# A chunk-selected attention and a gated feed-forward on one core: every engine's order written by a list scheduler, the feed-forward spread between heads, transposes by DMA later on, triangles on GpSimd

## The chip, the cores and the metric

The kernel runs on one core of one Trainium2 chip. The metric is the time of one execution in microseconds (us) on the device; smaller is better. Below, PE is TensorE, ACT ScalarE, DVE VectorE, POOL GpSimd and SP SyncE. PSUM is the memory that PE writes; it has eight banks of 512 float32 per partition, and no DMA and no POOL instruction touches it.

## The reference

Four batches, eight heads, 768 positions, head size 64. Each query takes the six best chunks of 32 keys, by an upper bound made of each chunk's smallest and largest key, and attends to them causally. The heads' outputs, side by side, are the input of a gated feed-forward layer that also mixes positions.

```python
B, H, S, D = q.shape                      # 4, 8, 768, 64
ub = np.sum(np.maximum(q[:, :, :, None, :] * k_min[:, :, None, :, :],
                       q[:, :, :, None, :] * k_max[:, :, None, :, :]), axis=-1)
top_chunks = np.argsort(ub, axis=-1)[..., -top_k:]          # 6 of 24, causal
scores = np.where(mask, scale * np.matmul(q, k.transpose(0, 1, 3, 2)), -1e9)
attn = softmax(scores);  x = heads side by side of attn @ v  # 768 x 512 a batch
h = np.maximum(x @ w_in, 0.0);  u, v = h[..., :512], h[..., 512:]
v_s = np.einsum('ts,bsd->btd', w_spatial, norm(v)) + b_spatial[None, :, None]
out = (u * v_s) @ w_out                                      # float32
```

## The kernel before

Work goes by **pairs** of heads: 16 pairs, four to a batch, a pair being 128 partitions wide (two heads of 64). For pair `i` there are three steps in the code.

- `load(i)` (L133): six DMAs on POOL's queue, two each for k, q and v, converted to float16 on the way.
- `prep(i)` (L148): PE transposes k (L152); DVE takes each chunk's maximum and minimum out of PSUM (L155, L156); ACT copies the transposed k into `kh` (L157, L158), whose other rows hold a constant pattern (made by POOL, L93 to L97, and copied by DVE, L107) that turns a chunk's selection bit into a large negative score; POOL lays out the chunk bounds `km` (L161). PE transposes q (L167), DVE splits it into positive and negative part (L169, L170), PE multiplies the bounds (L177), and DVE adds the causal mask (L180), takes the eight largest of each row (L186) and writes a bit for each chunk that isn't chosen beside q (L189). PE transposes this again (L196), and DVE copies it out as `a` (L198).
- `attend(i)` (L204), for each head: scores `sc` in three groups of up to two banks (L213), each diagonal block with a second matmul (L216) that adds a triangle `tri`; ACT's exp for each group (L217); the product with v (L224); DVE's normalisation (L227, L228). Then PE transposes the pair's output and DVE copies it into `xT` (L234, L235).

The feed-forward of a batch is a list of 21 pieces (L272 to L343): six `v_piece` (L285, ACT Relu L287, DVE statistics L289, L290), the norm (L295 to L299), four `u_piece` (L310, L312), four `s_piece` (positions mixed L322, the bias as one more matmul L324, the gate L325) and six `o_piece` (L333, copy L336, store on SP L337). Its pieces are issued after the pairs of the next batch, a share after each pair, and the last batch's after everything (L349 to L369). Within these, the framework's own scheduler sets each engine's order.

Each engine runs its instructions strictly in that order, so what stands behind a waiting instruction waits too. POOL's queue holds the loads, the weights' loads (L247) and `km`; a DMA of that queue also waits for the one eight before it. PSUM is shared out as two double banks `sc`, two `tr` and two `acc`.

Of the kernel before, what the change touches and what calls it, by code (L numbers as in the profile page):

```python
# [20 lines left out]

STRIPS = [
# [3 lines left out]
]  # L26
WIDTHS = [1024, 1024, 640]
BASES = [0, 1024, 2048]
EW = 2688


def block_column(t, qi):
    for g, strips in enumerate(STRIPS):
        for (tt, q0, n, col, _) in strips:
            if tt == t and q0 <= qi * P < q0 + n:
                return BASES[g] + col + qi * P - q0
    raise KeyError((t, qi))
# [3 lines left out]
def kernel(  # L41
# [24 lines left out]
    mm = nc.tensor.matmul  # L66

    cp = ctx.enter_context(tc.tile_pool(name="const", bufs=1))
    ring = ctx.enter_context(tc.tile_pool(name="ring", bufs=1))
    sb = ctx.enter_context(tc.tile_pool(name="sb", bufs=2))  # L70
    ml = ctx.enter_context(tc.tile_pool(name="ml", bufs=2))
    ps_sc = ctx.enter_context(tc.psum_pool(name="ps_sc", bufs=2))
    ps_tr = ctx.enter_context(tc.psum_pool(name="ps_tr", bufs=2))
    ps_acc = ctx.enter_context(tc.psum_pool(name="ps_acc", bufs=2))

    def trans_tile():
        return ps_tr.tile([P, S], F16, tag="tr", name="tr")
# [6 lines left out]
    identity = cp.tile([P, P], F16)  # L84
    make_identity(nc, identity)


    NB = 3
    qs_ring, kh_ring, v_ring = [], [], []
    expand = []  # L90
    for hi in range(2):
        ex = cp.tile([P, S], F16, name=f"expand{hi}")
        nc.gpsimd.memset(ex, NEG)  # L93
        row0 = 0 if hi == 0 else D
        nc.gpsimd.affine_select(out=ex, in_=ex, compare_op=Alu.is_ge, fill=0.0,
                                base=CHUNK * row0, channel_multiplier=-CHUNK, pattern=[[1, S]])
        nc.gpsimd.affine_select(out=ex, in_=ex, compare_op=Alu.is_ge, fill=0.0,  # L97
                                base=CHUNK - 1 - CHUNK * row0, channel_multiplier=CHUNK, pattern=[[-1, S]])
        expand.append(ex)
    for i in range(NB):  # L100
        qs = ring.tile([P, NQT, 2, P], F16, name=f"qs{i}")
        nc.vector.memset(qs, 0.0)
        qs_ring.append(qs)
        kh = []
        for hi in range(2):
            t = ring.tile([P, S], F16, name=f"kh{i}_{hi}")
            nc.vector.tensor_copy(t, expand[hi])  # L107
            kh.append(t)
# [9 lines left out]
    cmask = cp.tile([P, CPT], F32)  # L120
    nc.gpsimd.memset(cmask, 0.0)
    nc.gpsimd.affine_select(out=cmask, in_=cmask, compare_op=Alu.is_ge, fill=-1e9,
                            base=0, channel_multiplier=1, pattern=[[-CHUNK, CPT]])
    hmask = cp.tile([P, 2], F16)
    nc.gpsimd.memset(hmask, 0.0)
    nc.gpsimd.memset(hmask[0:D, 0:1], 1.0)
    nc.gpsimd.memset(hmask[D:2 * D, 1:2], 1.0)
    eps_t = cp.tile([P, 1], F32)
    nc.vector.memset(eps_t, 1e-6)

    kv = {}

    def load(i):  # L133
        b, hp = divmod(i, HP)
        qs, vt = qs_ring[i % NB], v_ring[i % NB]
        kp = sb.tile([P, NQT, 2, D], F16, tag="kp", name="kp", bufs=3)
        for hi in range(2):
            h = 2 * hp + hi
            view = lambda a: a[b, h].rearrange("(so si) d -> si so d", si=P)
            nc.gpsimd.dma_start(out=kp[:, :, hi, :], in_=view(k))  # L140
            c0 = D if hi == 0 else 0
            nc.gpsimd.dma_start(out=qs[:, :, hi, c0:c0 + D], in_=view(q))
            nc.gpsimd.dma_start(out=vt[:, :, hi, 0:D], in_=view(v))
        kv[i] = kp

# [254 lines left out]
```

## Time and profile before

| | us |
|---|---|
| median of three runs | 291.32 |
| lowest and highest | 287.43 and 292.05 |
| span of the profiled execution, first to last instruction | 287.5 |

The profiled execution has no other time of its own than its span. Its busy shares are PE 77%, DVE 59%, ACT 54%, POOL 34%. A busy PE counts a matmul to its modelled end, 0.16 us or so after the next one could start, so PE's real work is read from the steps between the starts of matmuls that follow each other.

### The profile page before, as it was taken

How to read it: one execution, taken by the hardware profiler on the slowest of the kernel's cores; microseconds unless marked ns; L12 is line 12 of the kernel's file. 1: busy time of each engine (PE TensorE's matmuls, PEld its weight loads, DVE VectorE, ACT ScalarE, POOL GpSimd, SP SyncE). 2: the span in 40 equal slices, each digit the busy share in tenths (PEclk: the TensorE clock that was granted, in tenths of full speed). 3: DMA queues.
4: the chain of work that ended last, by engine and by line, in shares of the span. 5: the costliest groups of instructions: out<-in, count | busy, mean ns of one | idle time of the engine just before them, and what ended most of it. 6: DMA issues, size and time to landing. Idle time of an engine off the chain costs nothing.

```text
span 287.5 us, 5812 instructions
## 1 busy us (share of the span) xinstructions
PE 222.4 (77%) x2340; PEld 144.9 (50%) x2340; DVE 170.7 (59%) x498; ACT 154.3 (54%) x217; POOL 98.1 (34%) x150
## 2 busy tenths in 40 slices
PE   0037028787879798989798989978888989799994
PEld 0025016666655565655465656655546565544551
DVE  8337005888788875565579865474688654238330
ACT  1021405775785868146878674086878660656213
POOL 9995264546562434124243424051200000000000
PEclk9999758999999999999999999999999999999999
DMA  0999997879996667558984848079220000140005
GB/s 1 65 120 199 194 127 52 56 49 71 70 65 41 46 41 47 37 64 65 204 55 31 55 31 57 0 81 222 16 15 3 0 2 0 39 182 2 0 0 219
DMA packets 80590, 18.86 MB, mean 66 GB/s; under 512 B 75698, under 2 KB 76978, under 8 KB 80564
## 3 DMA queue, kind: packets, MB, share of 16 engines
q0 software_dynamic: 77104, 12.20, 57.3%
q1 hardware_dynamic: 3460, 6.30, 6.0%
q8 instruction: 18, 0.29, 0.4%
q14 instruction: 8, 0.07, 0.1%
HBM read 24.39 MB, written 6.29 MB: 107 GB/s over the span
## 4 chain that ended last, share of the span: by engine, by line
PE 50%; ACT 23%; DMA 8%; POOL 7%; DVE 7%; issue 3%; ACTq 0%; DVEq 0%; POOLq 0%
ACT e L217 13%; PE acc L322 11%; PE sc L213 7%; PE acc L310 7%; DMA w_out_sb<-in_moe_w_out_dram 6%; PE acc L224 5%; PE acc L333 5%; PE acc L285 5%; DVE stats L289 2%; PE tr L234 2%; POOL kp L140 2%; PE sc L216 2%; DMA out_dram<-o 2%; ACT uT L312 2%; PE acc L324 2%
## 5 line engine op out<-in xcount | busy, mean ns | idle before, releaser
L217 ACT ACTIVATE e<-sc 128x1024 f16<-128x1024 f32 (+1 forms) x96 | 84.0, 916 | 44.0 <-PE sc L216 42.9
L140 POOL DMA_DIRECT2D kp<-in_k_dram x32 | 26.7, 839 | 54.1 <-PE tr L152 48.0
L224 PEld LDWEIGHTS <-e 128*128 128x128 f16 x672 | 27.0, 98 | 31.3 <-ACT e L217 17.8
L216 PE MATMUL sc<-tri,identity 128*128 128x128 f16 x192 | 39.5, 222 | 0.0
L336 ACT COPY o<-acc 128x512 f32<-128x512 f32 x24 | 14.0, 585 | 46.9 <-PE acc L333 44.8
L322 PE MATMUL acc<-wsT,vn 128*128 128x512 f16 (+1 forms) x192 | 37.2, 325 | 0.4 <-ACT uT L312 0.2
L325 DVE TENSOR_TENSOR gT<-acc,uT 128x512 f16<-128x512 f32 (+1 forms) x32 | 17.8, 557 | 20.0 <-PE acc L324 18.8
L155 DVE TENSOR_REDUCE kmm<-tr 128x24 f16<-128x768 f16 x16 | 15.3, 953 | 20.4 <-PE tr L152 20.3
L322 PEld LDWEIGHTS <-vn 128*128 128x128 f16 x192 | 18.2, 98 | 12.2 <-issue 1.1
L310 PE MATMUL acc<-xT,w_in_sb 128*128 128x512 f16 (+1 forms) x128 | 23.4, 325 | 0.9 <-ACT uT L312 0.7
L333 PE MATMUL acc<-w_out_sb,gT 128*128 128x512 f16 x96 | 23.1, 378 | 0.4 <-ACT o L336 0.3
L216 PEld LDWEIGHTS <-identity 128*128 128x128 f16 x192 | 19.0, 99 | 7.4 <-issue 5.7
L285 PE MATMUL acc<-w_in_sb,xT 128*128 128x512 f16 x96 | 22.2, 379 | 0.0
L177 PE MATMUL acc<-km,rq 128*128 128x48 f16 x160 | 9.6, 188 | 15.9 <-POOL km L161 14.5
L152 PE MATMUL tr<-identity,kp 128*128 128x128 f16 x96 | 10.0, 229 | 14.7 <-DMA kp<-in_k_dram 14.6
L312 ACT ACTIVATE uT<-acc 128x512 f16<-128x512 f32 (+1 forms) x32 | 14.3, 488 | 12.4 <-PE acc L310 12.3
L289 DVE BATCH_NORM_STATS2 stats<-vraw 128x6 f32<-128x512 f32 x24 | 16.6, 694 | 6.1 <-ACT vraw L287 6.1
L227 DVE RECIPROCAL rec<-acc 128x6 f32<-128x6 f32 x32 | 6.1, 190 | 22.9 <-PE acc L224 22.9
L287 ACT ACTIVATE vraw<-acc 128x512 f32<-128x512 f32 x24 | 14.3, 597 | 9.6 <-PE acc L285 9.6
L180 DVE TENSOR_TENSOR acc<-acc,cmask 128x40 f32<-128x40 f32 x16 | 3.3, 208 | 25.6 <-PE acc L177 22.7
L161 POOL TENSOR_TENSOR km<-kmm,hmask 128x48 f16<-128x48 f16 x32 | 8.3, 276 | 26.3 <-DVE kmm L155 22.6
L310 PEld LDWEIGHTS <-w_in_sb 128*128 128x128 f16 x128 | 12.1, 97 | 9.7 <-issue 1.3
(236 smaller groups left out, 452.0 us busy)
## 6 DMA issues: line engine op xcount, KB each, us to landing
out_dram<-o SPq DMA_DIRECT2D x24, 256.0 KB, 2.0
kp<-in_k_dram POOLq DMA_DIRECT2D x32, 96.0 KB, 3.3
qs_90<-in_q_dram POOLq DMA_DIRECT2D x12, 96.0 KB, 3.3
vt_96<-in_v_dram POOLq DMA_DIRECT2D x12, 96.0 KB, 3.0
ws_raw<-in_moe_w_spatial_dram POOLq DMA_DIRECT2D x1, 1152.0 KB, 15.1
w_in_sb<-in_moe_w_in_dram POOLq DMA_DIRECT2D x1, 1024.0 KB, 10.3
qs_98<-in_q_dram POOLq DMA_DIRECT2D x10, 96.0 KB, 3.2
vt_104<-in_v_dram POOLq DMA_DIRECT2D x10, 96.0 KB, 3.1
```

Source lines behind the costliest of these rows:

```text
L140: nc.gpsimd.dma_start(out=kp[:, :, hi, :], in_=view(k))
L213: mm(sc[:, col:col + n], lhsT=kh[hi][:, t * P:(t + 1) * P], rhs=a[hi][:, q0:q0 + n], start=True, stop=not dg)
L216: mm(sc[:, col:col + P], lhsT=identity, rhs=tri, start=False, stop=True)
L217: nc.scalar.activation(out=e[:, BASES[g]:BASES[g] + WIDTHS[g]], in_=sc[:, 0:WIDTHS[g]], func=Act.Exp, scale=scale)
L224: mm(avv[:, qi, :], lhsT=e[:, c:c + P], rhs=vt[:, t, hi, 0:D + 1], start=(t == 0), stop=(t == qi))
L285: mm(hv, lhsT=x[:, ko, bi * P:(bi + 1) * P], rhs=w_in_sb[:, ko, DH:DFF], start=(ko == 0), stop=(ko == NDO - 1))
L289: nc.vector.bn_stats(stats, st["vraw"][:, bi, :])
L310: mm(hu[:, 0:t1 - t0], lhsT=w_in_sb[:, ko, db * P:(db + 1) * P], rhs=x[:, ko, t0:t1], start=(ko == 0), stop=(ko == NDO - 1))
L312: nc.scalar.activation(st["uT"][:, db, t0:t1], hu[:, 0:t1 - t0], func=Act.Relu)
L322: mm(vs[:, 0:t1 - t0], lhsT=st["vn"][:, si, db * P:(db + 1) * P], rhs=wsT[:, si, t0:t1], start=(si == 0), stop=False)
L325: nc.vector.tensor_tensor(st["gT"][:, db, t0:t1], in0=vs[:, 0:t1 - t0], in1=st["uT"][:, db, t0:t1], op=Alu.mult)
L333: mm(o_ps, lhsT=st["gT"][:, db, ti * P:(ti + 1) * P], rhs=w_out_sb[:, db, :], start=(db == 0), stop=(db == KO - 1))
```

## The change

The file is rewritten. What is computed stays; these are its parts.

1. **Order.** Each piece of work is an operation with an engine, a length, a key, and names that it reads and writes. `Schedule.run` plays them through with these lengths: again and again it takes, over all engines, the operation that can start first, and among equals the one with the smallest key. That sequence is then issued, and the framework keeps it (`manual_schedule`). Eight single PSUM banks are handed out by it, with at most 3 for scores, 2 for transposes, 1 for bounds, 2 for outputs and 3 for the feed-forward at a time.
2. **Keys.** Pair `i` attends at `10 i`, is prepared at `10 i - 14` (the first at -50) and loaded at `10 i - 30`; the feed-forward of the batch whose last pair is `i` has V from `10 i + 16`, U from `+ 22`, S and O from `+ 30`.
3. **Loads.** A pair has four DMAs in place of six (k and v of both heads in one), and they come first on POOL, ahead of the constants. The weights are cut in nine and get keys 22 to 32, between the loads of pairs 5 and 6.
4. **Constants.** The pattern is made by DVE from the identity; DVE copies it to the rings' 64 rows.
5. **prep.** ACT copies transposed k once, whole (L378); DVE takes maxima and minima by a tree of two halvings and a reduction of 8 (L382 to L389) and places k in `kh` by four copies (L403). `km` is four small copies (L395), on DVE for the first two pairs and on POOL after. From pair 5 on, `a` comes from one DMA transpose on SP (L452) in place of 12 PE transposes and two DVE copies.
6. **attend.** Scores go by six groups of one bank, exp by six instructions. From pair 4 on no triangle is added by PE; POOL zeroes the triangles after exp, two instructions for a head (L501). The product with v comes in two parts (12 and 9 matmuls), started once for the whole bank. For pairs 4 to 14 a DMA transpose on SP writes `xT` (L530).
7. **Feed-forward.** U, and the mixed v, are computed with positions on the partitions; so the bias is a scalar for each partition in the gate (L602), and the bias matmuls and their preparation go. The gated tile must then be transposed: by DMA on SP for batches 0 to 2 (L606), by PE and DVE for the last (L613, L615).

```diff
+            for e, lst in ready.items():
+                for (k, n, t, o) in lst:
...
+                    t = max(t, free[e])
+                    if t < INF and (best is None or (t, k, n) < best[:3]):
+                        best = (t, k, n, e, o)
...
+    TRI_POOL = 4
+    A_XBAR = 5
+    PRE = 14
+    X_XBAR = 4
+    G_XBAR = 3
...
-        nc.vector.tensor_reduce(kmm[:, 0, :], trc, axis=AX.X, op=Alu.max)
-        nc.vector.tensor_reduce(kmm[:, 1, :], trc, axis=AX.X, op=Alu.min, negate=True)
-        nc.scalar.copy(kh[0][D:2 * D, :], tr[0:D, :])
-        nc.scalar.copy(kh[1][0:D, :], tr[D:2 * D, :])
+        s.op("ACT", *act_cost(S), lambda: nc.scalar.copy(kT, bk.f16[:, 0:S]), key, r=[bk], w=[("kT", n2)], drop=bk)
+            s.op("DVE", 0.26, 0.38, lambda m=m, op=op: nc.vector.tensor_tensor(
+                t1[:, m], in0=kc[:, :, 0:16], in1=kc[:, :, 16:32], op=op), key, r=[("kT", n2)], w=[("t1", n2, m)])
...
+                s.op("DVE" if i < 2 else "POOL", 0.2, 0.26, spread, key, r=[("kmm", n2, 0), ("kmm", n2, 1), ("kmz", n2)],
...
+        if i >= A_XBAR:
+            s.op("SP", 2.7, 4.7, lambda: nc.sync.dma_start_transpose(
+                out=a.rearrange("p t h c -> p (t h) c"), in_=qs.rearrange("p t h c -> p (t h c)")),
...
-                    if dg:
-                        mm(sc[:, col:col + P], lhsT=identity, rhs=tri, start=False, stop=True)
+                            dg = i < TRI_POOL and q0 == t * P
...
+                    nc.gpsimd.affine_select(out=o, in_=o, compare_op=Alu.is_ge, fill=0.0, base=0,
+                                            channel_multiplier=-1, pattern=[[0, 3], [1, P]])
+                if i >= TRI_POOL:
+                    s.op("POOL", *pool(3 * P), tri, kk, w=[("e", ne, 3 * part + j) for j in range(3)])
...
-                    mm(vs[:, 0:t1 - t0], lhsT=brow_l, rhs=brow[:, t0:t1], start=False, stop=True)
+            s.op("DVE", 0.61, 0.70, lambda t=t, bk=bk, g=g: nc.vector.scalar_tensor_tensor(
+                out=g, in0=bk.f32, scalar=bcol[:, t:t + 1], in1=u_r[nu[t]], op0=Alu.add, op1=Alu.mult),
...
+            if b < G_XBAR:
+                s.op("SP", 0.95, 3.0, lambda g=g, gT=gT: nc.sync.dma_start_transpose(out=gT, in_=g), kk,
...
+    weight_ops([22, 23, 26, 27, 28, 29, 30, 31, 32])
     for i in range(NPAIR):
+        load_ops(i, -101 if i == 0 else 10 * i - 30)
+        prep_ops(i, 10 * i - (PRE if i else 50))
+        attend_ops(i, 10 * i)
...
+            mlp_ops(b, k0, k0 + 6, k0 + 14, 1.0)
```

On POOL near the start of the program before, right behind the loads of the three weights, the second `km` row of pair 0 and the first of pair 1 stand with ten loads (`kp`, `qs_...`, `vt_...`) between them.

```order
L161 TENSOR_TENSOR km<-kmm,hmask 128x48 [waits DVE_49]
L140 DMA kp<-in_k_dram 128x6x64 [waits DMASW7_49]
L142 DMA qs_106<-in_q_dram 128x6x64 [waits DMASW0_49]
L143 DMA vt_112<-in_v_dram 128x6x64 [waits DMASW1_49]
L140 DMA kp<-in_k_dram 128x6x64 [waits DMASW2_49]
L142 DMA qs_106<-in_q_dram 128x6x64 [waits DMASW3_49]
L143 DMA vt_112<-in_v_dram 128x6x64 [waits DMASW4_49]
L140 DMA kp<-in_k_dram 128x6x64 [waits DMASW5_49,PE_49]
L142 DMA qs_90<-in_q_dram 128x6x64 [waits DMASW6_49,PE_49]
L140 DMA kp<-in_k_dram 128x6x64 [waits DMASW7_49]
L142 DMA qs_90<-in_q_dram 128x6x64 [waits DMASW0_49,PE_49]
L161 TENSOR_TENSOR km<-kmm,hmask 128x48 [waits DVE_49]
```

On POOL at the start of the program after the change:

```order
L321 DMA kp_79<-in_k_dram 128x12x64
L325 DMA qs_82<-in_q_dram 128x6x64 x2
L328 DMA vt_86<-in_v_dram 128x12x64
L269 ISA
L269 AFFINE_SELECT identity<-identity 128x128 [waits DVE_49]
L295 AFFINE_SELECT cmask<-cmask 128x4 [waits DVE_49]
L283 AFFINE_SELECT tri<-tri 128x128 [waits DVE_49]
L321 DMA kp_80<-in_k_dram 128x12x64
L325 DMA qs_83<-in_q_dram 128x6x64 x2
L328 DMA vt_87<-in_v_dram 128x12x64
L321 DMA kp_81<-in_k_dram 128x12x64 [waits DMASW0_49]
```

The loads of pairs 0 to 2 lead, and no `km` of pairs 0 and 1 is left on POOL; the weights follow after these rows.

On ACT where a batch's feed-forward runs beside pairs, before (`e` is exp of a head, `vraw` Relu of V, `kh` the copies of k):

```order
L217 ACTIVATE e<-sc 128x640
L287 ACTIVATE vraw<-acc 128x512
L217 ACTIVATE e<-sc 128x1024
L287 ACTIVATE vraw<-acc 128x512 x5
L217 ACTIVATE e<-sc 128x1024
L217 ACTIVATE e<-sc 128x640
L157 COPY kh_0_100<-tr 64x768
L158 COPY kh_1_102<-tr 64x768
```

And after (`u` is Relu of U, `rs` the norm):

```order
L588 ACTIVATE u_148<-bank_63 128x512
L493 ACTIVATE e_113<-bank_67 128x512
L493 ACTIVATE e_113<-bank_62 128x512
L493 ACTIVATE e_113<-bank_64 128x512
L493 ACTIVATE e_113<-bank_61 128x512
L588 ACTIVATE u_149<-bank_65 128x512
L493 ACTIVATE e_113<-bank_63 128x512
L568 ACTIVATE rs_143<-mv_139,eps 128x3
L493 ACTIVATE e_113<-bank_62 128x128
L570 ACTIVATE rs_143<-rs_143 128x3
L588 ACTIVATE u_150<-bank_66 128x512
```

The feed-forward's pieces come by ones and twos among a head's six exps, where five stood in one block.

On SP from the program's start, as one piece of the difference (`a` of pairs 5 to 7, `xT` of pairs 4 to 6, `gT` of batch 0); the two rows with a minus are all of SP's DMAs before, the bias and the stores:

```order
-L252 DMA bt<-in_moe_b_spatial_dram 1x768 x2
-L337 DMA out_dram<-o 128x512 x24
-L395 UNCONDITIONAL_BRANCH
+L667 UNCONDITIONAL_BRANCH
+L303 DMA bcol<-in_moe_b_spatial_dram 128x6x1
+L452 DMA_TRANSPOSE a_109<-qs_83 128x12x128
+L530 DMA_TRANSPOSE xT_122<-x_119 128x6x128
+L452 DMA_TRANSPOSE a_107<-qs_84 128x12x128
+L530 DMA_TRANSPOSE xT_122<-x_120 128x6x128
+L606 DMA_TRANSPOSE gT_164<-g_160 128x4x128
+L606 DMA_TRANSPOSE gT_165<-g_161 128x4x128
+L452 DMA_TRANSPOSE a_108<-qs_85 128x12x128
```

Forty transposes (11 of `a`, 11 of `xT`, 18 of `gT`) now stand in one queue with the 24 stores.

## Rows read from the trace of the kernel before

**Rows 1.** Busy time by stretch: start us:end us, length, engines' busy us (instructions), clock, DMA.

```profile
0.00:42.00 42.00, 8.66 (x66) 6.14 (x67) 16.00 (x42) 7.21 (x8) 30.94 (x50) 0.88 1.21 118
42.00:86.00 44.00, 36.13 (x549) 28.10 (x549) 33.90 (x114) 30.22 (x35) 24.07 (x35) 0.96 0.94 62
86.00:146.30 60.30, 53.17 (x567) 34.51 (x565) 39.72 (x118) 37.95 (x54) 21.56 (x33) 1.00 0.68 65
146.30:206.40 60.10, 53.49 (x578) 34.80 (x576) 39.77 (x118) 38.16 (x55) 19.68 (x29) 1.00 0.64 64
206.40:256.20 49.80, 44.89 (x450) 28.25 (x449) 29.01 (x80) 29.17 (x44) 1.88 (x5) 1.00 0.11 22
256.20:287.60 31.40, 26.04 (x136) 13.05 (x134) 12.33 (x26) 11.56 (x23) 0.00 (x0) 1.00 0.20 73
```

**Rows 2.** PE in order of time, first 42 us: start us, us, what [idle before <- releaser].

```profile
14.60 0.80 PE L152 MATMUL tr<-identity,kp 128*128 128x128 f16 x6 [14.60 <-DMA kp<-in_k_dram]
...
25.57 0.63 PE L213 MATMUL sc<-a_213,kh_0_92 128*128 128x512 f16 x1
...
40.09 0.20 PE L177 MATMUL acc<-km,rq 128*128 128x48 f16 x1 [11.01 <-POOL km L161]
```

**Rows 3.** POOL in order of time, first 42 us.

```profile
11.01 0.84 POOL L140 DMA_DIRECT2D kp<-in_k_dram  x1
...
28.88 0.82 POOL L143 DMA_DIRECT2D vt_112<-in_v_dram  x1 [3.48 <-DMA w_in_sb<-in_moe_w_in_dram]
35.13 0.83 POOL L140 DMA_DIRECT2D kp<-in_k_dram  x1 [5.43 <-DMA ws_raw<-in_moe_w_spatial_dram]
```

**Rows 4.** Chain that ended last, 40 to 60 us: start us, us, what.

```profile
53.62 0.24 PE acc L177 x9
...
54.12 0.92 DVE max_444 L186 x10
...
56.27 0.64 PE acc L224 x21
...
58.32 0.34 PE tr L258 x6
```

**Rows 5.** The same chain, 252 us to the end.

```profile
256.18 5.20 PE acc L285 x24
...
272.28 0.70 DVE gT L325
...
278.07 5.46 PE acc L333 x24
```

**Rows 6.** The same chain, 86 to 146 us: ACT.

```profile
92.80 2.54 ACT e L217 x3
95.36 0.79 ACT kh_0_92 L157
```

**Rows 7.** DVE: one group of lines (busy us, mean ns), and two copies in order of time.

```profile
L155 DVE TENSOR_REDUCE kmm<-tr 128x24 f16<-128x768 f16 x16 | 15.3, 953 | 20.4 <-PE tr L152 20.3
...
6.76 0.89 DVE L107 COPY kh_0_92<-expand_82 128x768 f16<-128x768 f16 x1
...
9.23 0.34 DVE L107 COPY kh_1_110<-expand_86 128x768 f16<-128x768 f16 x1
```

**Rows 8.** Busy time of one early stretch, columns as in rows 1.

```profile
1.00:6.75 5.75, 0.00 (x0) 0.00 (x0) 5.33 (x14) 1.10 (x1) 5.71 (x9) 1.00 0.00 1
```

**Rows 9.** POOL, the same instruction twice: groups of lines.

```profile
L97 POOL TENSOR_SCALAR_AFFINE_SELECT expand_86<-expand_86 128x768 f16<-128x768 f16 x1 | 1.6, 1569 | 0.0
...
L97 POOL TENSOR_SCALAR_AFFINE_SELECT expand_82<-expand_82 128x768 f16<-128x768 f16 x1 | 0.8, 816 | 0.0
```

**Rows 10.** DMA issues: queue, count, KB each, median us from issue to landing.

```profile
out_dram<-o SPq DMA_DIRECT2D x24, 256.0 KB, 2.0
kp<-in_k_dram POOLq DMA_DIRECT2D x32, 96.0 KB, 3.3
...
w_out_sb<-in_moe_w_out_dram POOLq DMA_DIRECT2D x1, 512.0 KB, 16.9
```

More of the change, by code (lines that the diff above doesn't have):

```diff
@@ L6 @@
 from concourse import bass_utils, mybir
-from concourse.masks import make_identity
 from concourse._compat import with_exitstack
@@ L22 @@
 STRIPS = [
[3 rows of a table removed]
-]
-WIDTHS = [1024, 1024, 640]
-BASES = [0, 1024, 2048]
+    [(0, 0, 512, 0)],
+    [(1, 128, 512, 0)],
+    [(2, 256, 512, 0)],
+    [(0, 512, 256, 0), (4, 512, 256, 256)],
+    [(1, 640, 128, 0), (3, 384, 384, 128)],
+    [(5, 640, 128, 0)],
+]
+WIDTHS = [512, 512, 512, 512, 512, 128]
+BASES = [0, 512, 1024, 1536, 2048, 2560]
 EW = 2688
[L32 to L37, printed above, removed]
+DIAGS = [(0, 512), (1792, 384)]
@@ new lines, in blocks, with __init__, f32, f16 @@
+def blocks(groups):
+    out = []
+    for g in groups:
+        for (t, q0, n, col) in STRIPS[g]:
+            for j in range(n // P):
+                out.append((t, q0 // P + j, BASES[g] + col + j * P))
+    return out
+class Bank:
+    def __init__(self, cls):
+        self.cls, self.tile = cls, None
+    @property
+    def f32(self):
+        return self.tile[:, :]
+    @property
+    def f16(self):
+        return self.tile[:, :].bitcast(F16)
+class Op:
+    __slots__ = ("eng", "occ", "vis", "emit", "key", "take", "drop", "deps", "left", "users", "start", "end",
+                 "seen", "load", "n", "tag")
@@ L40, with pe_cost, act_cost, dve_cost @@
+MM = 1 / 2400.0
+def pe_cost(ns):
+    occ = sum(n * MM + 0.0027 for n in ns)
+    return occ, occ + 0.22
+def act_cost(n):
+    return n / 1200.0 + 0.085, n / 1200.0 + 0.22
+def dve_cost(n, rate=0.96, fixed=0.06):
+    return n / (rate * 1000.0) + fixed, n / (rate * 1000.0) + fixed + 0.13
 @with_exitstack
@@ L126 @@
[L126 to L133, printed above, removed]
+    W = 2 * NCH
+    TRI_POOL = 4
[3 more added lines that the diff above has]
+    G_XBAR = 3
+    cp = ctx.enter_context(tc.tile_pool(name="const", bufs=1))
+    pp = ctx.enter_context(tc.psum_pool(name="psum", bufs=1))
+    banks = [pp.tile([P, 512], F32, name=f"bank{j}") for j in range(8)]
+    s = Schedule(banks, {"sc": 3, "tr": 2, "ub": 1, "av": 2, "mlp": 3})
@@ new lines, in ring @@
+    def ring(n, shape, dt, name):
+        return [cp.tile(shape, dt, name=f"{name}{j}") for j in range(n)]
+    identity = cp.tile([P, P], F16, name="identity")
+    ex = cp.tile([D, S], F16, name="ex")
+    cmask = cp.tile([P, CPT], F32, name="cmask")
+    tri_t = cp.tile([P, P], F16, name="tri")
+    eps_t = cp.tile([P, 1], F32, name="eps")
+    bcol = cp.tile([P, NQT], F32, name="bcol")
+    w_in_sb = cp.tile([P, NDO, DFF], F16, name="w_in")
+    w_out_sb = cp.tile([P, KO, DM], F16, name="w_out")
@@ new lines, in spatial_ops, with tr @@
+    def spatial_ops(key):
+        for so in range(NQT):
+            bk = Bank("tr")
+            def tr(so=so, bk=bk):
+                for to in range(NQT):
+                    nc.tensor.transpose(bk.f16[:, to * P:(to + 1) * P], ws_raw[:, to, so * P:(so + 1) * P], identity)
+            s.op("PE", *pe_cost([P] * NQT), tr, key + 0.1 * so, r=["identity"] + [("ws", to) for to in range(NQT)],
+                 take=bk, w=[bk])
+            s.op("DVE", 0.474, 0.58, lambda so=so, bk=bk: nc.vector.tensor_copy(wsT[:, so, :], bk.f16[:, 0:S]),
+                 key + 0.1 * so, r=[bk], w=[("wsT", so)], drop=bk)
```

667 lines of the change are left out of this document (419 added, 248 removed), and 3 rows, old and new, of the table STRIPS.

## The prediction

> **What bounds the kernel now.** I read the stretches first, because one share of busy time over 288 us hides that this kernel has stages with different limits [rows 1]. The cuts are where the feed-forward of a batch begins (its V matmuls, L285). Until 42 us PE is busy for 8.7 us; until 86 us four pairs are done without any feed-forward beside them, PE busy 36.1 of 44, DVE 33.9; then two batches of 60 us each with PE busy 53 of 60, a third of 49.8, and a tail of 31.4 us that holds the last feed-forward alone.
>
> Second, the start, in order of time. PE begins at 14.60 us, since the second half of k is issued by POOL at 11.01 us, behind constants and other loads; the first score comes at 25.57; and at 40.09 PE ends a wait of 11.01 us for `km` of pair 1 [rows 2, 3]. POOL was late with it because loads stand ahead of it, and those waited 3.48 and 5.43 us for two of the weights' loads [rows 3].
>
> Third, what PE does when it is busy, read from steps in the chain: a 512-column matmul takes 5.20/24 = 0.217 us, a 128-column one 0.34/6 = 0.057, one of 65 columns (product with v) 0.64/21 = 0.030, one of 48 (bounds) 0.24/9 = 0.027 [rows 4, 5]. With 256 columns at 0.109 and 384 at 0.163 (by columns), a pair before costs: scores 2 x (3 x 0.217 + 2 x 0.109 + 0.163 + 2 x 0.057) = 2.3, product with v 42 x 0.030 = 1.3, bounds 0.3, and 42 of 128 columns (12 for k and q, 12 for `a`, 12 triangles, 6 for `xT`) = 2.4; together 6.3. A feed-forward costs V and O 24 x 0.217 = 5.2 each, U 16 x (0.217 + 0.109) = 5.2, mixing 24 x 0.326 = 7.8, bias 8 matmuls = 1.3; together 24.7. A batch is 4 x 6.3 + 24.7 = 49.9 us of PE in a stretch of 60.2, so some 10.3 us of each stretch are stalls. So PE bounds the batches, DVE and POOL's queue the first 86 us.
>
> **PE's work after the change.** It loses 12 triangles a pair from pair 4 (0.7), 12 transposes for `a` from pair 5 (0.7), 6 for `xT` except in pairs 0 to 3 and 15 (0.35), and the bias. A late pair costs 2.3 + 1.3 + 0.3 + 0.7 = 4.6 us, a feed-forward 5.2 x 3 + 36 x 0.217 = 23.4. Over the program: before 16 x 6.3 + 4 x 24.7 + 2 (w_spatial) = 202; after 16 x 4.6 + 2.7 (triangles of 4 pairs) + 3.4 (`a` of 5) + 1.7 (`xT` of 5) + 93.6 + 1.4 (24 gate transposes) + 2 = 178. That is 24 us less; the rest of what goes must be waiting.
>
> **Start and first four pairs: 56 us in place of 86.** The loads lead POOL's queue. From issue to PE took 11.01 to 14.60 = 3.6 us with the second half of k [rows 2, 3]; a load with twice the pieces, issued at about 1 us, I put at 5, so work on k starts at 6 us. `km` of pairs 0 and 1 is DVE's, so the 11 us wait is gone. What is late next is DVE. Its busy time until 86 us was 16.00 + 33.90 = 49.9 [rows 1]. Off go 19.9 us: twelve reductions of 0.953 = 11.4, the pattern's six copies of 0.34 to 0.89, 3.2 [rows 7], and the presets and bias preparation, 5.3 [rows 8]. On come, for six preparations, the tree and four placing copies, which no row shows. For the tree, at L155's rate its 2304 elements in six instructions give 2.5 us; with the four halvings at the rate of the fast copy, 768 columns in 0.34 [rows 7], 1.5; I take 1.6, since the halvings are float16 in SBUF as that copy is. The four copies are 0.8 at the 0.34 rate and 1.8 at the 0.89 rate; I take 0.8, by the same likeness. That is 6 x 2.4 = 14.4; presets, pattern and `km` at the same rates come to 6.4. DVE has 49.9 - 19.9 + 20.8 = 50.8, of it 3 before k lands: 47.8 after 6 us. Before, it was busy 77% of the second stretch (33.9 of 44); with an order chosen for it I take 95%: 6 + 50 = 56. Bounds: 52, with part of the last preparation left for later; 75 at 77% and both slow prices (6 x 1.9 more).
>
> **Pairs 4 to 15 with three feed-forwards: 132 us in place of 170.** By then PE has done 31 us (k, q and bounds of six preparations, 5.7; `a` of five, 3.4; the rest of four pairs, 18.6; w_spatial 2; V's first matmuls 1.3). The last feed-forward takes 24 more, so 178 - 31 - 24 = 123 us remain here. Other engines: ACT's three exps of 2688 columns take 2.54 [rows 6], that is 0.1 us for each instruction beside the columns, so six take 2.84; with one copy of k for two (0.79 each) a pair costs 6.5 us of ACT, as before. DVE keeps near 39.7 of a 60 us stretch [rows 1]: dropped copies of `a` and `xT` pay for the placing copies. POOL was busy 21.6 and gains four selects a pair. So PE stays the bound, but V can't begin before the batch's last `xT`, and about a pair in each batch runs without filler at ACT's 6.5 instead of PE's 4.6: 2 us. For waits in a static order I add 1 us a batch: 123 + 9 = 132. Bounds: 123; and 123 + 3 x 10.3 = 154 if the stalls stay as they are.
>
> The DMA transposes are the new wait. No row shows one. Below stands a store from SP, 2.0 us; above, a load queued behind megabytes, 16.9; I take 4, near the loads' 3.3 [rows 10]. What hides it: in the order, 7 to 12 us of PE's work stand between pair i's bounds and its first score, and DVE needs some 1.5 of that (the eight largest take 0.92 [rows 4], mask and bits stand around them), so 4 us cost nothing; past 8 us every further us costs 11 us over the program. A late transpose holds the stores and transposes behind it in SP's queue, and PE at O, V and scores; a store that waits for ACT's copy of O holds the `a` behind it in the same way, which the same 4 us of slack must cover. Below nothing I exclude: PE's share of it is counted above. A select costs nothing at best, as PE has scores in between, and at most the slow case under the rivals; I take nothing.
>
> **Tail: 29.5 us in place of 31.4.** 24 us of PE, the gate's transposes in it; 1.5 from the last product with v to V (divide, transpose, copy, half of it under V's first matmuls); then copy and store as now, 287.5 - 283.5 = 4 [rows 5]. The stalls for ACT between U's tiles and DVE's 0.70 gates [rows 5] are filled by the next tile, with more banks.
>
> **Sum.** 56 + 132 + 29.5 = 217.5, against the profiled span of 287.5. That span lies at the lowest of the three runs and 1.3% under their median, so the median forecast is 217.5 x 291.32/287.5 = **220 us**. Its own range is 210 to 230. A difference under 2% is about what a measurement here can't tell from none.
>
> **Rivals.**
> *Fewer stalls.* DVE at 52 us and 1 us lost a batch: 52 + 126 + 29 = 207, or 210 us. For it: many fillers are ready at once. Against: each engine's order was fixed with assumed lengths.
> *The stalls stay.* PE waits 10.3 us a batch because an exp, a tree or a norm lands later than the order assumes, and nothing behind it can go ahead: 56 + 154 + 29.5 = 239.5, or 243. For it: the order puts an output's matmul right at the moment its exp should end. Against: much of today's stall is blocks of feed-forward that push exps back.
> *POOL's triangles are late.* The same POOL instruction on 768 columns took 816 ns once and 1569 once, the second beside DVE's two-input work and copies [rows 9]. A select of 384 columns is then 0.41 to 0.78 us by halves. Two a head in 24 heads come to 48 x 0.78 = 37 us if nothing covers them, and 19 with every other one behind scores or filler: 236.5, or 240. A select can also stand behind a load that waits for a free buffer, since POOL's queue is one. Against: three scores or a filler usually stand before the product, and half the time the short case holds. The Trainium skill ("SBUF — State Buffer", Who interferes with whom) speaks against this part of the change: VectorE and GpSimd share a port pair, and copies in a two-port mode, or two SBUF inputs, block the other engine for a whole instruction. The trace agrees with it as far as one pair of rows can, and by the rule the change adds on both sides, placing copies on DVE and selects on POOL.
> *Transposes on SP are slow; slower than before.* If one takes 13 us, `a` costs 11 x (13 - 8) = 55, and V and O wait 9 us longer than the 4 of my forecast in three batches, 54, of which the pairs' own matmuls cover about half: 217.5 + 55 + 27 = 299.5, or 303. From about 12.5 us it is more than 2% slower than before; at 9 to 12 us the time lies between 240 and 292. For it: forty in one queue beside the loads, and 16.9 us does occur [rows 10]. Against: that was a load queued behind two larger ones, and the weights are in by then.
>
> **How the numbers follow.** Forecast 0.47; fewer stalls 0.15; stalls stay 0.18; triangles late 0.08; transposes slow but not slower than before 0.06, of it 0.02 within 2%; slower 0.06. So faster 0.92, same 0.02, slower 0.06. The range of 204 to 246 holds the forecast, fewer stalls, stalls stay and late triangles, each but for its edges: 0.83.
>
> **What would show it.** Right: first score near 14 us and the rest of V near 56; about 44 us between the V of two batches; PE's total busy under 205; a DMA transpose landing within 5 us; no long wait of PE for POOL. Wrong: PE waiting for `a` or `gT` in each pair; DVE at 100% past 60 us; selects of 1 us with PE's product behind them. A batch stretch over 50 us falsifies the middle term, that V after 65 the first.

## The result and the profile after

| | us |
|---|---|
| before, median of 4 runs (lowest, highest) | 291.69 (287.43, 293.13) |
| after, median of 4 runs (lowest, highest) | 238.19 (237.00, 240.76) |
| ratio after to before, 95% interval | 0.820 (0.809 to 0.831) |
| span of the profiled execution after | 235.0 |

The ratios, here and below, leave out runs that are over 1.5% longer than the fastest of their kernel at a lower granted clock, and the medians don't; the profiled run of e5, below, is such a one (285.9 us at 0.673), so its stretches are read from e9, the same kernel.

The kernel is faster by 18%. The forecast was 220 us; of the 17.5 us by which the span exceeds the 217.5 forecast, the stretches below show the place. They are those of [rows 1] cut where the changed kernel's stages meet: first score, the rest of the first V, two batches, the third, the tail. Columns are the same: start:end, length, busy us of PE, weight loads, DVE, ACT and POOL, then clock, DMA share and GB/s. The DMA share adds up the time that packets took, over 16 engines, so it can pass 1.

```profile
0.00:18.00 18.00, 5.08 (x46) 4.17 (x47) 13.47 (x55) 2.88 (x3) 16.82 (x24) 1.00 1.77 112
18.00:58.50 40.50, 35.69 (x528) 27.43 (x528) 39.47 (x160) 30.17 (x61) 26.90 (x46) 1.00 1.70 155
58.50:112.00 53.50, 44.35 (x444) 25.62 (x442) 40.99 (x146) 37.13 (x78) 27.97 (x50) 1.00 1.27 130
112.00:167.50 55.50, 49.44 (x477) 28.34 (x478) 44.25 (x163) 37.64 (x80) 25.17 (x54) 0.94 1.01 128
167.50:205.00 37.50, 34.77 (x295) 18.84 (x294) 19.53 (x53) 25.60 (x55) 6.00 (x12) 1.00 0.45 100
205.00:235.00 30.00, 25.27 (x125) 11.39 (x123) 14.18 (x30) 11.21 (x22) 0.00 (x0) 0.94 0.14 53
```

Start and first four pairs end at 58.5 us (forecast 56), the tail takes 30.0 (forecast 29.5), and between them lie 146.5 us where 132 were forecast. There PE is busy 44.35 + 49.44 + 34.77 = 128.6 us and idle for 17.9.

PE in order of time, as in [rows 2] (start us, us, what, [idle before <- what ended it]): the wait for `km` of pair 0, the first score, the first full V matmuls, and the same point one batch and two batches later.

```profile
10.97 0.20 PE L425 MATMUL bank<-km,rq 128*128 128x48 f16 x1 [3.05 <-DVE km L395]
...
18.05 0.59 PE L486 MATMUL bank<-a,kh 128*128 128x512 f16 x1 [1.40 <-DVE a L464]
...
60.06 1.24 PE L557 MATMUL bank<-w_in,xT 128*128 128x512 f16 x5
...
111.91 0.39 PE L557 MATMUL bank<-w_in,xT 128*128 128x512 f16 x1 [3.04 <-DMA xT<-x]
...
168.58 2.75 PE L557 MATMUL bank<-w_in,xT 128*128 128x512 f16 x12
```

So 52 to 57 us pass between the V of two batches, not 44. What ends PE's waits from 58 to 206 us, and SP's longest over the whole span (what waited, for what: us in total, times, longest):

```profile
PE bank L620 <- DMA gT<-g: 7.0, 8, 2.4
...
PE bank L557 <- DMA xT<-x: 3.0, 1, 3.0
...
PE bank L425 <- DVE x L522: 2.0, 1, 2.0
...
PE bank L425 <- POOL km L395: 1.4, 3, 0.8
...
PE bank L510 <- POOL e L501: 0.6, 2, 0.5
```

```profile
SPq L625 <- ACT o L623: 39.8, 15, 19.5
```

Ten of the idle 17.9 us end with a DMA transpose's landing, of `gT` before O and once of `xT` before V. POOL's triangles cost PE 0.6 us. The 3.04 us wait is followed by a stretch at the lower of PE's two clock levels, with PE busy all through (columns as above; 0.50 is 1.2 GHz):

```profile
110.00:112.00 2.00, 0.09 (x1) 0.09 (x2) 1.31 (x6) 0.00 (x0) 0.00 (x0) 1.00 2.15 151
112.00:114.00 2.00, 2.00 (x22) 1.25 (x23) 0.44 (x1) 1.24 (x4) 0.52 (x1) 0.81 1.58 157
114.00:116.00 2.00, 2.00 (x22) 1.68 (x20) 0.63 (x4) 1.30 (x3) 1.25 (x2) 0.50 0.35 78
116.00:118.00 2.00, 2.00 (x19) 0.90 (x17) 1.60 (x3) 0.66 (x2) 1.88 (x5) 0.84 1.44 95
```

These rows lose 2 x (0.19 + 0.50 + 0.16) = 1.7 us of work; the whole stretch from 112 to 167.5, with mean 0.94, loses 55.5 x 0.06 = 3.3. The rest of it lies at 164 to 168 us (0.61 and 0.54), behind the 2.0 us wait for DVE's `x`, which is no transpose.

The groups that answer to [rows 7, 9] (busy us, mean ns | idle before):

```profile
L501 POOL TENSOR_SCALAR_AFFINE_SELECT e<-e 128x384 f16<-128x384 f16 x48 | 25.3, 529 | 69.2 <-ACT e L493 68.8
...
L403 DVE COPY kh<-kT 64x384 f16<-64x384 f16 x64 | 22.2, 347 | 1.2
```

The DMA queues of the whole execution (packets, MB, share of 16 engines), POOL's first; the second holds SP's transposes and stores:

```profile
q0 software_dynamic: 77200, 12.19, 71.7%
q1 hardware_dynamic: 40080, 15.15, 32.5%
```

And its DMA issues, columns as in [rows 10]:

```profile
kp<-in_k_dram POOLq DMA_DIRECT2D x16, 192.0 KB, 5.0
...
gT<-g SPq DMA_TRANSPOSE x18, 2.5
```

The median transpose is quick, the slowest are not: `gT` lands in 2.4 to 6.0 us (median 2.5), `xT` in 2.8 to 7.3 (4.9), `a` in 3.7 to 5.8 (4.5). Two views of the DMAs issued in a short stretch show when. From 104 to 112 us, with a pair's loads on their way:

```profile
q0 software_dynamic: 3896, 0.49, 115.1%
...
kp<-in_k_dram POOLq DMA_DIRECT2D x1, 192.0 KB, 8.7
...
xT<-x SPq DMA_TRANSPOSE x1, 7.3
```

From 183 to 200 us, when all loads are done:

```profile
q1 hardware_dynamic: 5837, 2.56, 56.7%
...
gT<-g SPq DMA_TRANSPOSE x6, 2.4
...
xT<-x SPq DMA_TRANSPOSE x1, 2.8
```

### The profile page after: what moved, and what is told of

Its sections match the earlier page's. It is cut to its first block, busy times and chain, and to the rows that moved or that the text cites. A ratio compares the mean times of both kernels' runs of the same rounds, so it can differ in the third digit from the quotient of the medians.

```text
span 235.0 us, 5366 instructions
## 1 busy us (share of the span) xinstructions
PE 194.6 (83%) x1910; PEld 115.8 (49%) x1910; DVE 171.9 (73%) x604; ACT 144.6 (62%) x297; POOL 102.9 (44%) x184
## 5 line engine op out<-in xcount | busy, mean ns | idle before, releaser
L493 ACT ACTIVATE e<-bank 128x512 f16<-128x512 f32 x192 | 93.0, 554 | 26.4 <-PE bank L486 13.6
L486 PE MATMUL bank<-a,kh 128*128 128x512 f16 (+3 forms) x256 | 58.2, 312 | 3.9 <-DVE a L464 2.1
L501 POOL TENSOR_SCALAR_AFFINE_SELECT e<-e 128x384 f16<-128x384 f16 x48 | 25.3, 529 | 69.2 <-ACT e L493 68.8
L598 PE MATMUL bank<-vn,wsT 128*128 128x512 f16 x144 | 37.2, 379 | 0.0
L510 PE MATMUL bank<-vt,e 128*128 128x65 f16 x672 | 32.4, 194 | 1.0 <-POOL e L501 0.6
L486 PEld LDWEIGHTS <-kh 128*128 128x128 f16 x256 | 23.0, 99 | 17.3 <-issue 3.6
L602 DVE SCALAR_TENSOR_TENSOR g<-bank,bcol,u 128x512 f16<-128x512 f32 x24 | 17.9, 748 | 17.4 <-PE bank L598 15.5
L557 PE MATMUL bank<-w_in,xT 128*128 128x512 f16 x96 | 27.7, 419 | 3.6 <-DMA xT<-x 3.0
L620 PE MATMUL bank<-w_out,gT 128*128 128x512 f16 x96 | 23.9, 380 | 7.6 <-DMA gT<-g 7.0
L325 POOL DMA_DIRECT2D qs<-in_q_dram x32 | 26.7, 848 | 2.3 <-DMA a<-qs 2.1
L584 PE MATMUL bank<-w_in,xT 128*128 128x512 f16 x96 | 24.3, 379 | 0.0
L403 DVE COPY kh<-kT 64x384 f16<-64x384 f16 x64 | 22.2, 347 | 1.2
L378 ACT COPY kT<-bank 128x768 f16<-128x768 f16 x16 | 13.1, 821 | 10.8 <-PE bank L376 10.0
L518 DVE RECIPROCAL rec<-bank 128x6 f32<-128x6 f32 x32 | 6.0, 186 | 18.1 <-PE bank L510 17.9
```

What stands on the lines that cost most here:

```text
L325: s.op("POOL", 0.84, 0, lambda hi=hi, c0=c0: nc.gpsimd.dma_start(out=qs[:, :, hi, c0:c0 + D], in_=one(q, hi)), key + 0.1, w=[("qd", i % le ...
L403: nc.vector.tensor_copy(o, f)
L486: mm(bs.f32[:, col:col + n], lhsT=kh[:, hi, t * P:(t + 1) * P], rhs=af[:, q0 // P:(q0 + n) // P, :], start=True, stop=not dg)
L493: s.op("ACT", *act_cost(WIDTHS[g]), lambda g=g, bs=bs, e=e: nc.scalar.activation(out=e[:, BASES[g]:BASES[g] + WIDTHS[g]], in_=bs.f32[:, 0: ...
L501: nc.gpsimd.affine_select(out=o, in_=o, compare_op=Alu.is_ge, fill=0.0, base=0, channel_multiplier=-1, pattern=[[0, 3], [1, P]])
L510: mm(o[:, qi, :], lhsT=e[:, c:c + P], rhs=vt[:, hi, t, 0:D + 1], start=(part == 0 and n == 0), stop=(part == 1 and n == len(bl) - 1))
```

## The experiments

Three theories on the 10 us of waits and what hangs on them. **Q**: SP issues transposes and stores in one order, and a store that waits for ACT (39.8 us of SP's waits) holds the transposes behind it. **C**: the transposes are issued in time, but land late because they share the DMA engines with a pair's loads. **L**: the schedule's lengths are too short (a placing copy 0.16 us, measured 0.347), so every engine's order fits badly. Q and L were stated before e1, C only after e4. All times in the table are medians; the ratio is to the kernel before, run beside it; "idle" is PE's idle time from 60 to 180 us of the profiled execution, 120 less its busy time in that one stretch (the same stretch isn't the same work).

| run | change to the changed kernel | us | ratio, 95% | idle |
|---|---|---|---|---|
| after | none | 238.2 | 0.809 to 0.831 | 15.2 |
| e1 | stores issued by ACT | 244.1 | 0.834 to 0.847 | 19.7 |
| e2 | measured lengths | 232.3 | 0.791 to 0.807 | 13.4 |
| e3 | `gT` on PE for all batches | 229.1 | 0.782 to 0.795 | 8.1 |
| e4 | feed-forward in one block | 249.7 | 0.856 to 0.868 | 22.1 |
| e5 | no loads of pairs 6 to 15 | 226.3 | 0.770 to 0.785 | |
| e6 | all transposes on PE | 236.0 | 0.807 to 0.821 | 6.1 |
| e7 | all triangles on PE | 237.5 | 0.808 to 0.825 | 12.2 |
| e8 | weights loaded early | 247.4 | 0.844 to 0.861 | 18.7 |
| e9 | e5 once more, a single run | 224.8 | | 6.4 |
| e10 | e5 and e3 together | 224.9 | 0.771 to 0.783 | 5.8 |
| e11 | e3, last `xT` on PE, some copies on ACT | 216.4 | 0.742 to 0.752 | 3.3 |
| e12 | e11 and e2 together | 224.3 | 0.759 to 0.773 | 5.8 |

**e1, stores from ACT.**

```diff
-            s.op("SP", 0.1, 2.2, lambda t=t, o_sb=o_sb: nc.sync.dma_start(out=out[b, t * P:(t + 1) * P, :], in_=o_sb),
+            s.op("ACT", 0.1, 2.2, lambda t=t, o_sb=o_sb: nc.scalar.dma_start(out=out[b, t * P:(t + 1) * P, :], in_=o_sb),
```

> The 24 stores of the output are issued by ACT instead of SP, nothing else. Theory Q (SP's queue): between 58.5 and 205 us TensorE waits 7.0 us for gT and 3.0 us for xT because SP issues its transposes in order behind stores that wait for ACT (39.8 us of SP's waits); without the stores these 10 us fall to about 4, at least one of the two half-clock stretches in the middle goes, and the time comes to 228 to 233 us against 238.2. Theory L (lengths): the order was laid out with lengths shorter than the chip's (a placing copy 0.16 us against 0.35), so each engine runs late at other places as well; then the waits move and the time stays within 236 to 240. A store costs ACT some 0.1 to 0.5 us, 2 to 12 us in all on an engine that is 62% busy.

It got slower, 244.1 us, and PE's waits for `gT` and `xT` grew from 10.0 to 12.7 us (58 to 206 us). SP's queue in order of time, then PE's wait:

```profile
89.51 3.57 SPq L606 DMA_TRANSPOSE gT<-g  x2
93.29 4.15 SPq L452 DMA_TRANSPOSE a<-qs  x1
```

```profile
98.01 1.89 PE L620 MATMUL bank<-w_out,gT 128*128 128x512 f16 x4 [5.51 <-DMA gT<-g]
```

Nothing stands ahead of these two `gT` in SP's queue, they are issued from 89.51, and PE gets the one it needs at 98.01 (the longest landing of a `gT` in this run is 8.5 us). Theory Q falls as the main cause. The Trainium skill ("DMA: Bandwidth & Descriptors", Issuing engines are not separate DMA queues) states that DMAs run on the same 16 engines and interleave, whichever engine issues them. The trace agrees, 5.51 us of waiting with the stores on another queue. Why it is slower than the changed kernel and not the same wasn't taken further; the granted clock from 58.5 to 205 us is 0.95 in place of 0.98.

Q keeps a share. In the changed kernel three of the eight waits for `gT`, 3.6 of the 7.0 us, are for one that SP issued 1.1 to 1.8 us after its `g` was done, behind a store or another transpose. The longest of them, DVE's `g`, SP's two issues and PE's wait:

```profile
82.30 0.75 DVE L602 SCALAR_TENSOR_TENSOR g<-bank,bcol,u 128x512 f16<-128x512 f32 x1 [0.27 <-PE bank L598]
84.42 0.35 SPq L625 DMA_DIRECT2D out_dram<-o  x1
84.87 1.21 SPq L606 DMA_TRANSPOSE gT<-g  x1
90.53 1.04 PE L620 MATMUL bank<-w_out,gT 128*128 128x512 f16 x4 [2.42 <-DMA gT<-g]
```

Issued at once, and with the same time to landing, these three would have cost 3.0 us less at most (an estimate, 1.8 + 0.6 + 0.5). The other five, and the `xT` that cost 3.04 us, were issued within 0.03 us of their data.

**e2, measured lengths.** Ten operations get measured lengths, one of them so:

```diff
-                s.op("DVE", 0.16, 0.28, put, key + 3, r=[("kT", n2)], w=[("kh", nh, hi, par)])
+                s.op("DVE", 0.36, 0.47, put, key + 3, r=[("kT", n2)], w=[("kh", nh, hi, par)])
```

> Only the lengths by which the schedule is laid out are changed to those of the trace (placing copy 0.36 for 0.16, V statistics and g 0.65 and 0.68, key and value loads 1.05, transposes by DMA landing 4.9, 5.2 and 3.2 us after issue, a store 0.55 on SP); the work is the same. Theory L: TensorE's idle time between 58.5 and 205 us falls from 18 to about 9 us and the time to 226 to 231 us. Theory Q: SP still carries everything in order, the idle time stays at 15 us or more and the time at 234 to 240.

232.3 us lies between the two ranges; the idle time from 58.5 to 205 us, 15.1 us, is what Q expected. PE's waits, 58 to 206 us:

```profile
PE bank L620 <- DMA gT<-g: 7.3, 5, 4.4
PE bank L486 <- DMA a<-qs: 2.2, 1, 2.2
```

The waits for `gT` are as large as before, with other rows hit. These lengths don't cure a landing of `gT` that is 2.4 us at one time and 9.4 at another (this run's longest).

**e3, `gT` on PE.** `G_XBAR = 0` in place of 3.

> g of batches 0 to 2 is transposed by TensorE and copied by VectorE, as in the tail, and no more by DMA. Theory Q: the 7.0 us of waits for gT go and SP is freer (18 transposes of 1.2 us fewer), against 18 x 0.3 us of TensorE and 18 x 0.42 us of VectorE: 5.4 us more work, so 234 to 239 us. Theory L: the new pair of steps per row of O runs into VectorE, which is 78% busy there, and TensorE waits for the copies instead: 240 to 245 us.

229.1 us, better than any theory expected, with 72 more matmuls on PE and 18 more copies on DVE. Ahead the stretch with batch 0's O in the changed kernel, behind it the same stretch in e3:

```profile
80.00:100.00 20.00, 15.70 (x145) 8.60 (x144) 11.54 (x41) 10.10 (x21) 6.62 (x13) 1.00 1.39 179
```

```profile
80.00:100.00 20.00, 19.32 (x189) 11.06 (x190) 14.37 (x54) 12.52 (x26) 8.88 (x16) 1.00 1.53 155
```

3.6 us of the 9 are in these 20 us, and the mean granted clock of the execution rises from 0.978 to 0.993.

**e4, no spreading.**

```diff
-            mlp_ops(b, k0, k0 + 6, k0 + 14, 1.0)
+            mlp_ops(b, 10 * i + 7, 10 * i + 7.2, 10 * i + 7.4, 0.01)
```

> The keys put a batch's feed-forward in front of the next pairs' attention instead of spreading it between them; all else is as in the changed kernel. If the spreading is what gives TensorE its filler, pairs 4 to 15 lose it: ACT's exponentials (93 us of them) bound the pairs, some 20 us of ACT per batch are no longer covered, and the time comes to 250 to 262 us. If the spreading gives little, the time stays within 235 to 242.

249.7 us, at the edge of what was expected: the spreading is worth 11.5 us. V then follows its last `xT` at once and waits 8.5 us for it in all, so part of these 11.5 is again a transpose's landing.

**e5, e9 and e10, no later loads.** The loads of pairs 6 to 15 are left out, so these pairs compute on the data of earlier ones; the order of all else is the same. The first of three such calls (q's stands for two loads):

```diff
-        s.op("POOL", 0.84, 0, lambda: nc.gpsimd.dma_start(out=kp, in_=view(k)), key,
+        s.op("POOL", 0.84, 0, lambda: i < 6 and nc.gpsimd.dma_start(out=kp, in_=view(k)), key,
...
```

> The loads of q, k and v of pairs 6 to 15 are left out (these pairs work on what pairs 2 to 5 left in the buffers); every other instruction stands where it stood on its engine, all 40 DMA transposes included. Theory C (contention): a transpose lands late because its small packets share the 16 DMA engines with a pair's loads; without them gT lands in 2.4 to 2.6 us and xT in about 2.8 each time, TensorE's 10 us of waits for them between 58.5 and 205 us go, with the half-clock stretches behind them, and the time is 224 to 229 us. Theory Q (SP's order) keeps most of these waits, as stores and transposes are issued in the same order as before: 234 to 238 us.

> The same kernel as e5 (loads of q, k and v of pairs 6 to 15 left out), once more for a profile at full granted clock. Theory C: gT lands in 2.4 to 2.6 us and xT in about 2.8 at the median; TensorE waits under 2 us for both between 58.5 and 205 us, against 10.0 in the changed kernel; idle time there 6 to 9 us against 18. Theory Q: the waits for transposes are still 5 us or more.

226.3 us in the first, 224.8 in the second. In e9 `xT` lands in 2.7 to 3.1 us (median 2.7), `a` in 3.6 to 5.6 (3.7), `gT` in 2.4 to 4.5 (2.5), and of the ten us that PE waited for `gT` and `xT` this is left:

```profile
PE bank L620 <- DMA gT<-g: 2.8, 4, 1.2
```

Between 58 and 206 us PE idles for 9.2 us in place of 17.9. Nothing in SP's order changed. The 2.8 us lie between what C expected (under 2) and what Q did (5 or more), and 1.8 of them are for two `gT` that SP issued 1.0 and 2.1 us after their `g`. The lower clock didn't go with the waits: the granted clock from 58.5 to 205 us is 0.98 in both. So theory C stands for the larger part. That loads make transposes late is shown by leaving them out; that they do it by filling the DMA engines is read from the shares above (115.1% and 57.9% from 104 to 112 us).

> Loads of pairs 6 to 15 left out and gT of all batches on TensorE. With the loads, gT on TensorE saved 9 us (238.2 to 229.1). Theory C: without the loads there is no wait left to save, and the 5.4 us of TensorE's transposes remain: 226 to 231 us, the same as or slower than e5's 226.3. If a DMA transpose costs the same whatever else the DMA engines carry, this run saves another 9 us: 216 to 220.

224.9 us: without the loads, `gT` on PE changes the time by 1.4 us, inside the intervals; with them it changes it by 9. It is just under what C expected (226 to 231) and far from 216 to 220. So the DMA transpose isn't dear by itself, it is dear beside loads. Leaving the loads out also frees POOL of 40 issues, and PE's waits for POOL were 2.0 us in all.

**e6, all transposes on PE.** `G_XBAR = 0`, `X_XBAR = 16`, `A_XBAR = 16`.

> a, xT and gT of all pairs and batches are transposed by TensorE and copied by VectorE. Against the run with gT alone on TensorE (229.1 us) this adds 11 x 12 + 11 x 6 transposes at .34 us per six, 11 us of TensorE, and 33 copies of 0.47 us, 15.5 us of VectorE, and takes away 2 us of waits for xT. Theory C expects 236 to 242 us: the transposes of a and xT have slack and earn their place on the DMA, only gT's did not. If every DMA transpose costs more than it saves, it is 222 to 229 us.

236.0 us, at the lower end of what C expected: `a` and `xT` on the DMA earn 7 us against e3, `gT` loses 9, and the three together bring the changed kernel nothing that can be told from no change. The Trainium skill's rule ("VectorE: DVE Perf Modes", Rules for kernel authors) is to transpose on TensorE where PSUM will do as the destination, and by DMA otherwise. For `gT` the runs agree (9 us), for `a` and `xT` they don't (7 us the other way). The likely reason is how much other work PE has before it needs the result; no run tests this apart.

**e7, triangles on PE.** `TRI_POOL = 16`.

> The diagonal masks of all pairs are added by TensorE again (144 matmuls more of about 0.06 us a step, 8 to 9 us) and POOL's 48 selects (25.3 us) go. If the selects lie off the path, as predicted, the time is 242 to 247 us; if they hold the second product back, the time is 232 to 238.

237.5 us lies in the range that was expected if the selects hold the product back (232 to 238). The rows give another reason, since PE waited only 0.6 us for the selects. The middle, in the changed kernel and in e7, and e7's longest wait of PE in it:

```profile
58.50:205.00 146.50, 128.56 (x1214) 72.80 (x1212) 104.77 (x361) 100.37 (x212) 59.15 (x115) 0.98 0.96 122
```

```profile
58.50:205.00 146.50, 132.42 (x1353) 80.26 (x1351) 101.84 (x361) 101.35 (x214) 34.88 (x69) 0.99 0.97 120
```

```profile
PE bank L620 <- DMA gT<-g: 10.4, 8, 3.8
```

PE does 139 more matmuls in the same stretch and is idle 3.9 us less: it fills time in which it would have waited. This is read from the rows; no run has the triangles on PE and no waits for `gT`.

**e8, weights early.** Keys -50 to -46 in place of 22 to 32.

> The nine weight loads (some 5 MB) are issued ahead of the loads of pairs 1 to 3, as in the kernel before. If the later weight loads are what brought the start forward, the fourth pair's scores and the V matmuls come later by 8 to 16 us, and the time is 246 to 254 us; if VectorE binds the start whatever is loaded when, the time stays at 236 to 241.

247.4 us, as expected: V's first matmul starts at 50.7 us in place of 39.6 (the changed kernel, then e8).

```profile
39.60 0.59 PE L557 MATMUL bank<-w_in,xT 128*128 128x512 f16 x2
```

```profile
50.71 0.59 PE L557 MATMUL bank<-w_in,xT 128*128 128x512 f16 x2
```

**e11 and e12, towards a better kernel.**

```diff
-    G_XBAR = 3
+    G_XBAR = 0
...
-                    nc.vector.tensor_copy(o, f)
-                s.op("DVE", 0.16, 0.28, put, key + 3, r=[("kT", n2)], w=[("kh", nh, hi, par)])
+                    if hi == 0 and i < 6:
+                        nc.scalar.copy(o, f)
+                    else:
+                        nc.vector.tensor_copy(o, f)
+                onact = hi == 0 and i < 6
+                s.op("ACT" if onact else "DVE", 0.40 if onact else 0.36, 0.53 if onact else 0.47, put, key + 3, r=[("kT", n2)], w=[("kh", nh, hi, par)])
...
-        if i >= X_XBAR and i < NPAIR - 1:
+        if i >= X_XBAR and i % HP < HP - 1:
```

> On top of e3 (gT on TensorE): x of the last pair of each batch is transposed on TensorE too (removes 1.7 us of waits for xT, adds 3 x 0.34 us of TensorE), and of the first six pairs one head's two placing copies go to ACT (12 copies of 0.35 us leave VectorE, which was 97% busy from 18 to 58.5 us; the first score is not touched). Expected: the V matmuls that follow the first pairs start about 3 us earlier, 225 to 228 us against 229.1. If VectorE did not bind the first stage, 229 to 231.

The diff also gives the 52 copies that stay on DVE their measured length, which the expectation doesn't say. 216.4 us (216.3 to 216.9), far better than expected, and 9% under the changed kernel. Busy time by stretch in e11:

```profile
0.00:60.00 60.00, 46.46 (x627) 35.29 (x628) 53.31 (x217) 43.89 (x87) 49.37 (x79) 1.00 1.80 146
60.00:180.00 120.00, 116.67 (x1175) 69.25 (x1175) 101.62 (x359) 90.93 (x192) 51.74 (x103) 1.00 0.92 117
```

and its two longest waits of PE between 58.5 and 190 us:

```profile
PE bank L429 <- POOL km L395: 0.9, 2, 0.5
PE bank L542 <- DVE x L526: 0.5, 1, 0.5
```

In the first 60 us PE gets 3.9 us more done than in e3 (46.46 against 42.52), as the relief of DVE was meant to do; in the next 120 it is idle 4.7 us less (3.3 against 8.1). Of the 12.7 us between the two profiled spans (227.9 and 215.2) PE's busy time makes up another 3.5 (196.3 against 192.9 us, the mean granted clock rising from 0.993 to 1.000) and its idle time after 180 us 0.6. Which of the edits, the length among them, brought which part is open, since they ran together.

> e11 with the schedule's lengths set to the trace's (as in e2). The lengths alone were worth 6 us (238.2 to 232.3), most of it where gT was late; with gT on TensorE that part is gone, so 0 to 4 us: 223 to 227 us. If the lengths were worth 6 us by themselves, 219 to 222.

224.3 us lies in the expected range, but that was worked out from e3's 229.1. Against e11 it is slower: by the ratios, 0.766 and 0.747, some 5.5 us. PE's longest waits from 58 to 190 us are now for POOL's selects:

```profile
PE bank L514 <- POOL e L505: 3.5, 4, 1.5
```

So a schedule with truer lengths is not better in itself. Theory L isn't excluded as a part: e2 alone gained 6 us, and e11 has the copy's measured length.

## Why the prediction was right, and what it missed

The direction and the range of 204 to 246 held; the forecast's own range of 210 to 230 did not. PE as the bound of the batches and DVE as that of the start were right. That 238 us lies inside the wide range is in part luck: it lies near the rivals of late triangles (240) and of stalls that stay (243), but what made it longest was slow transposes, and that rival had 240 us and more. By its steps:

- **Start.** Right in kind, 2.5 us short. The first score comes at 18.05 us (forecast 14), V at 58.5 (56), DVE is busy 39.47 of 40.5 us, as assumed. Part of the 4 us of the first score is `km` of pair 0, whose four copies take DVE 1.9 us (9.03 to 10.92) while PE waits. For the whole stage the mis-sized term is the four placing copies: 4 x 0.347 = 1.39 us a preparation in place of 0.8, that is 6 x 0.59 = 3.5 us; the tree is (10.7 + 7.8 + 9.8)/16 = 1.8 against 1.6. By the fast row of [rows 7] 768 columns take 0.34 us, and here 384 do; why is open. Two bounds of this step don't come out of their terms, though the forecast doesn't use them: 2304 elements at L155's rate are 2.9 us, not 2.5, and 6 + (47.8 + 6 x 1.9)/0.77 is 83 us, not 75. e8 shows that loading the weights late is worth 9 us over the whole time, and e11 speaks for DVE as the limit there, as far as its edits can be told apart.
- **PE's work.** PE's busy time is 194.6 us, under the 205 named. But the saving that came from moving work off PE was counted at full value, and e6 and e7 show that it had none as made: 144 triangles (8 us at 0.057) or 270 transposes (15 us) could each be given back to PE without making the time longer. By the rows of e7, what was saved on PE was spent on waiting.
- **The middle, 132 us.** The step that failed is "For waits in a static order I add 1 us a batch", with the transposes' "4 us cost nothing" behind it. The batch stretches of over 50 us that were to falsify it came. For `a`, the one transpose whose slack was worked out, the step held: it lands in 4.5 us at the median and PE never waits for it. `gT` and the batch's last `xT` were given the same slack without a count. With loads beside them they land up to 6.0 and 7.3 us after issue. PE waited 10.0 us for them, up to 3.0 of it by SP's order. The 14.5 us by which the middle is longer are 8.9 of idle time (17.9 against 9), 3.3 at the lower clock, 1.7 of it behind the wait for `xT`, and 2.3 of busy time (128.6 less the 3.3, against 123; a busy PE counts matmuls to their modelled ends). e5 takes the loads away and e3 takes `gT` off the DMA; they bring the whole time down by 12 and 9 us.
- **Tail.** 30.0 us against 29.5, by luck in part: with a mean granted clock of 0.94 it loses 30 x 0.06 = 1.8 us, which the forecast doesn't have.
- **Rivals.** Late triangles: no, the selects took 0.53 us at the mean and PE waited 0.6 us for them; 0.51 to 0.70 us for each of 48 speaks against a shared port as a large cost in this mix. The Trainium skill's rule ("SBUF — State Buffer", Who interferes with whom), that VectorE and GpSimd lock a shared port pair against each other for a whole instruction, isn't tested by it. Slow transposes: the right place and far the wrong size, 10 us over the three batches where that rival had 13 us for each transpose. Stalls stay: 17.9 us of idle time in the three batches against that rival's 31, so the change removed some of it.

The rewrite as a whole gains by its parts as follows, each from a run that undoes it: spreading 11.5 us, later weight loads 9; triangles on POOL none that can be told from no change, and the DMA transposes, all three kinds together, none either. The start's `km` and loads (from 25.57 to 18.05 us at the first score) and the order itself weren't undone one by one.

## What to carry to other kernels

Price a DMA by how long it takes beside the other traffic of that stretch, not by its median, and count, for each place that waits for it, the work that stands between issue and use. Work taken off the busiest engine is worth only what that engine doesn't then wait; put it back as a test before believing the gain. In a statically ordered kernel, move the dependence that varies most (here one transpose) to an engine whose time is steady, even at the price of more work.

## What the runs showed of the hardware that was not expected

Taking ten pairs' loads away brought the landing of the `xT` transposes from a median of 4.9 us (up to 7.3) to 2.7 (up to 3.1), though the transposes were issued in the same order by the same engine. And a placing copy of 64x384 float16 values takes DVE 347 ns (334 to 352) with POOL's selects in the program and 348 (333 to 351) in e7 without them, and ACT 509 ns in e11:

```profile
L404 ACT COPY kh<-kT 64x384 f16<-64x384 f16 x12 | 6.1, 509 | 0.3
```
